# Moving the six groups of the transposed second matrix from batches 1 and 2 to batches 2 and 3

## The chip, the core and the metric

The kernel runs on one core of a Trainium2 chip. The time is the device time of one execution in microseconds (us); smaller is better. A core has the engines TensorE (PE), VectorE (DVE), ScalarE (ACT), GpSimd (POOL) and SyncE (SP, which issues most DMAs). Each works off its own queue in the order in which the program was written out; an instruction whose inputs are not there yet holds all behind it on that engine. The on-chip memories are SBUF and, for the results of matmuls, PSUM with 8 banks.

## The reference

```python
# 4 batches x 12 heads x 448 tokens x 64; scores are passed through a sigmoid, not a softmax
scores = (q @ k.T) / sqrt(64) - log(448);   x = sigmoid(scores) @ v        # x: 1792 tokens x 768
h = x @ w_in;   g = where(h > 0, h, exp(min(h, 0)) - 1);   x2 = g @ w_out   # w_in 768x2048, w_out 2048x768
logits = x2 @ w_gate                                                        # 8 experts, 224 tokens for each
for idx in argsort(-logits.flatten()):   # the largest logit takes its token, until an expert is full
    ...
out[tokens of e] = relu(x2[tokens of e] @ w1[e]) @ w2[e]
```

The choice of experts needs the logits of all tokens, so it can begin only when the last batch's are known.

## The kernel before

**Numbers.** Every fp32 operand of a large product is split into a high part `h` and a rest `l`, and a product is three matmuls (h with h, h with l, l with h). DVE makes the rest by a subtraction; the cast that makes the high part goes to ACT or DVE. The weights come as pairs of 32-bit words of fp64 numbers; a few bit operations on DVE and one scaling pass on ACT `join` a pair into one fp32 word.

**Stages.** The four batches (448 tokens each) go through `attention(b)`, `layer1(b)` and `layer2(b)`. The program issues `layer1(b)`, then `attention(b + 1)`, then `layer2(b)`, and the attention of the next batch is interleaved with both layers; behind `layer1(3)` there is no further attention. `layer1` has 16 steps f: the split of one block of `w_in` (128x768), 18 matmuls of 448 columns into one PSUM bank, then the elu of the result: `Exp` and `Tanh` on ACT, two operations on DVE of which the second is the last that reads the bank, then the split of the result into `gH` and `gL`. `layer2` has 6 blocks of 48 matmuls. In batch 0 the weights are joined and stored (`wcopy`); the later batches load the joined ones.

**The transposed second matrix.** For the last batch the logits are not taken from `x2` but earlier, from `gH` and `gL` and the product of `w_out` and `w_gate` (`wgs2`), in `last_logits()`. That product is built by `through(k)`, six groups for k = 0 to 5. A group loads two halves of `w_outT[k]` (1 MB each) into the two tiles `arena0` and `arena1`, joins each half in place, takes a bank from the ring of `layer1`, runs four fp32 products with `wgp` as the stationary operand (8 matmul records), and adds the bank to the accumulator `acc`. For each half:

```python
plan.dma(x, w_outT[k, hf])
V.tensor_scalar(lo, lo, 29, None, op0=ALU.logical_shift_right)
V.scalar_tensor_tensor(out=lo, in0=hi, scalar=-0x80000000, in1=lo, ...)
A.activation(f32(hi), f32(hi), AF.Copy, scale=2.0 ** -112)
V.tensor_scalar(hi, hi, 0x0FFFFFFF, 3, op0=ALU.bitwise_and, ...)
V.tensor_tensor(out=y, in0=hi, in1=lo, op=ALU.bitwise_or)
```

The last group (k = 5) is followed by four transposes into a further bank and the split into `wgs2`. The two arenas hold one group at a time, so the loads of the next group wait for the matmuls of the last. After the last group the arenas hold the tables of the expert search (`tables()`).

**Banks.** `mm` is a ring of three PSUM banks, 0, 1 and 2: each call gives the next in turn, to a step f, to a group, and to the transposes. A bank is written again only when what was in it has been read.

**What sets the order.** All operations are recorded, and a planner (`Plan.run`) writes out one queue for each engine: it takes operations by their estimated start and, where they could start together, by priority, which is the place in the program unless `plan.first(n)` moves it. The loads and joins of a group have `first(-300)`, which puts them behind their neighbours; `last_logits`, `tables`, `search` have `first(1e5)`. The order on the engines is fixed from then on.

Of the kernel before, what the change touches and what calls it, by code (L numbers as in the profile page):

```python
# [44 lines left out]
def f32(ap):  # L45
    return ap.bitcast(F32)
# [244 lines left out]
def kernel(  # L291
# [97 lines left out]
    def hcopy(dst, src):  # L389
        AV_.copy(dst, src)  # L390

    def lsub(dst, src, h):
        V.tensor_tensor(out=dst, in0=src, in1=f32(h), op=ALU.subtract)
# [68 lines left out]
    def through(k):  # L462


        ws = []
        for hf in range(2):
            x = r_raw()
            if wide:
                y = x.rearrange("p a b -> p (a b)")[:, :KH * P].rearrange("p (a b) -> p a b", b=P)
                lo, hi = (x.rearrange("p c (f two) -> p c f two", two=2)[:, :, :, i] for i in range(2))  # L470
                with plan.first(-300):
                    plan.dma(x, w_outT[k, hf])
                    V.tensor_scalar(lo, lo, 29, None, op0=ALU.logical_shift_right)
                    V.scalar_tensor_tensor(out=lo, in0=hi, scalar=-0x80000000, in1=lo, op0=ALU.bitwise_and,
                                           op1=ALU.bitwise_or)
                    A.activation(f32(hi), f32(hi), AF.Copy, scale=2.0 ** -112)
                    V.tensor_scalar(hi, hi, 0x0FFFFFFF, 3, op0=ALU.bitwise_and, op1=ALU.logical_shift_left)
                    V.tensor_tensor(out=y, in0=hi, in1=lo, op=ALU.bitwise_or)
                y = f32(y)
            else:  # L480
                y = x.rearrange("p a b -> p (a b)")[:, :KH * P].rearrange("p (a b) -> p a b", b=P).bitcast(F32)
                plan.dma(y, w_outT[k, hf])
            ws.append(y.rearrange("p a b -> p (a b)"))
        ps = mm()
        with plan.unit():
            for j in range(4):
                PE.matmul(ps[32 * j:32 * j + 32, :4 * P], wgp[:, k, :], ws[j // 2][:, j % 2 * 4 * P:(j % 2 + 1) * 4 * P],
                          start=True, stop=True)
        if k == 0:
            V.tensor_copy(acc, ps)  # L490
        else:
            V.tensor_tensor(out=acc, in0=ps, in1=acc, op=ALU.add)
        if k == KD - 1:
            ps = mm()
            with plan.unit():
                for c in range(4):
                    PE.transpose(ps[:, c * P:(c + 1) * P], acc[:, c * P:(c + 1) * P], ident)
            src = ps.rearrange("p (c j x) -> p j c x", j=4, x=32)[:, :, :, :E]
            w4 = wgs2.rearrange("p (j c) x -> p j c x", j=4)
            V.tensor_copy(w4[:, :, :, :E], src)  # L500
            lsub(w4[:, :, :, E:], src, w4[:, :, :, :E])

    def weights(b, r):

        n = KD if r < KF else KH
        src = w_in[r] if r < KF else w_out[r - KF]
        d = r_wd()
        if wide and b == 0:
            x = r_raw()
            plan.dma(x[:, :n], src)  # L510
            join(d[:, :n], x[:, :n], d[:, :n])
            plan.dma(wcopy[r, :, :n], d[:, :n])
        else:
            plan.dma(d[:, :n], wcopy[r, :, :n] if wide else src)
        h, l = r_wh(), r_wl()
        hcopy(h[:, :n], d[:, :n])
        lsub(l[:, :n], d[:, :n], h[:, :n])
        return h, l
# [65 lines left out]
    def layer1(b):  # L584
        ws = {}
        for f in range(-2, KF):
            with plan.first(200), plan.after(xs[0][GW + f][0]) if b == 0 and f < 1 else nullcontext():
                if f + 2 < KF:
                    ws[f + 2] = weights(b, f + 2)
            if f < 0:  # L590
                continue
            if b in (1, 2) and f in (1, 6, 11):
                through((b - 1) * 3 + f // 5)
            h, l = ws.pop(f)
            ps = mm()
            for c in range(KD):
                with plan.unit():
                    for n, (w, m) in enumerate(((h, 0), (h, 1), (l, 0))):
                        PE.matmul(ps[:, :S], w[:, c, :], xs[b][c][m], start=c == 0 and n == 0,
                                  stop=c == KD - 1 and n == 2)  # L600
            e, t = r_a(), r_a()
            A.activation(e, ps[:, :S], AF.Exp)
            A.activation(t, ps[:, :S], AF.Tanh, scale=0.5)
            V.scalar_tensor_tensor(out=t, in0=e, scalar=1.0, in1=t, op0=ALU.add, op1=ALU.mult)
            V.scalar_tensor_tensor(out=t, in0=t, scalar=0.0, in1=ps[:, :S], op0=ALU.min, op1=ALU.max)
            hcopy(gH[:, f, :], t)
            lsub(gL[:, f, :], t, gH[:, f, :])
# [82 lines left out]
    for b in range(B):  # L690
        plan.bias = BIAS[1] if b == 0 else {}
        layer1(b)
        if b == 0:
            plan.dma(wg, w_gate.rearrange("(d p) e -> p d e", p=P))
            V.tensor_copy(wgs[:, :, :E], wg)
            lsub(wgs[:, :, E:], wg, wgs[:, :, :E])
            V.memset(wgp, 0.0)
            V.tensor_copy(wgp[:, :, :E], wg)
        plan.bias = BIAS[2] if b == 0 else {}
        if b + 1 < B:  # L700
            attention(b + 1)
        layer2(b)
# [403 lines left out]
```

## Time and profile before

| | |
|---|---|
| median of 3 runs | 1009.49 us (1008.43 to 1009.92) |
| profiled execution | 1010.62 us, of it the span 1008.8 us |
| busy: PE, weight loads, DVE, ACT | 97%, 80%, 75%, 44% of the span |
| mean granted clock of TensorE | 0.990 |
| `layer1` of batch 3 on PE | 562.7 to 615.7 us |

The span runs from the first instruction to the last. A row that says "idle before, releaser" tells how long the engine stood in front of that work and which engine's work ended the wait. A matmul record is about 366 ns long in `layer1`, but the matmuls overlap, so that 261 of them take 53.17 us. The granted clock is 1.00 at full speed (2.4 GHz) and 0.50 at the lower level (1.2 GHz).

### The profile page before, as it was taken

How to read it: one execution, taken by the hardware profiler on the slowest of the kernel's cores; microseconds unless marked ns; L12 is line 12 of the kernel's file. 1: busy time of each engine (PE TensorE's matmuls, PEld its weight loads, DVE VectorE, ACT ScalarE, POOL GpSimd, SP SyncE). 2: the span in 40 equal slices, each digit the busy share in tenths (PEclk: the TensorE clock that was granted, in tenths of full speed). 3: DMA queues.
4: the chain of work that ended last, by engine and by line, in shares of the span. 5: the costliest groups of instructions: out<-in, count | busy, mean ns of one | idle time of the engine just before them, and what ended most of it. 6: DMA issues, size and time to landing. Idle time of an engine off the chain costs nothing. (4 is left out here: it accounts for less than half of the span.)

```text
span 1008.8 us, 15529 instructions
## 1 busy us (share of the span) xinstructions
PE 976.4 (97%) x6039; PEld 811.5 (80%) x6039; DVE 752.6 (75%) x1335; ACT 445.8 (44%) x631; POOL 45.6 (5%) x42
## 2 busy tenths in 40 slices
PE   8999999998999999899999999999899999999997
PEld 3497666786886698777678898888899989989997
DVE  5899977769996445997434687788798899798861
ACT  6779856446564412675320342133433244342320
POOL 0000000000000000000000000010011111102000
PEclk9999999999999999999999999999899999999999
DMA  7856767866452366433124333375555547456820
GB/s 218 294 201 237 264 229 265 271 230 213 175 203 86 115 171 198 164 115 111 63 79 138 113 115 105 120 252 185 174 208 174 187 137 278 163 168 239 282 89 28
DMA packets 63562, 177.99 MB, mean 176 GB/s; under 512 B 6336, under 2 KB 28096, under 8 KB 60416
## 3 DMA queue, kind: packets, MB, share of 16 engines
q1 hardware_dynamic: 60832, 165.98, 48.8%
q0 software_dynamic: 2656, 11.01, 3.5%
q8 instruction: 47, 0.77, 0.3%
q14 instruction: 27, 0.22, 0.1%
HBM read 147.87 MB, written 29.10 MB: 175 GB/s over the span
## 5 line engine op out<-in xcount | busy, mean ns | idle before, releaser
L247 PE MATMUL bank<-zone_r 128*128 128x448 f32 (+1 forms) x3384 | 633.7, 343 | 12.9 <-DVE zone L247 10.1
L247 PEld LDWEIGHTS bank<-zone_r 128*128 128x128 f32 x3384 | 556.3, 191 | 79.5 <-issue 20.6
L247 DVE TENSOR_TENSOR zone_r<-zone,zone_r 128x768 fp32r<-128x768 f32 (+3 forms) x347 | 314.3, 918 | 34.9 <-ACT zone_r L247 28.3
L247 PE MATMUL twin<-zone_r 128*112 128x384 f32 (+2 forms) x1416 | 226.2, 354 | 3.3 <-ACT zone L247 3.3
L247 PEld LDWEIGHTS twin<-zone_r 128*112 128x112 f32 (+2 forms) x1416 | 187.0, 175 | 33.4 <-issue 15.6
L247 ACT ACTIVATE zone_r<-zone 128x768 fp32r<-128x768 f32 (+3 forms) x194 | 151.6, 795 | 123.2 <-PE bank L247 48.6
L247 ACT ACTIVATE zone<-bank 128x448 f32<-128x448 f32 x156 | 79.5, 542 | 187.2 <-PE bank L247 161.0
L247 DVE CAST zone_r<-zone 128x768 fp32r<-128x768 f32 (+3 forms) x153 | 84.9, 557 | 91.0 <-PE bank L247 69.5
L247 ACT ACTIVATE zone<-twin,bias_s 112x896 f32<-112x896 f32 x96 | 92.8, 1005 | 61.5 <-PE twin L247 61.2
L247 PE MATMUL bank<-zone 112*64 112x448 f32 x384 | 83.9, 553 | 0.9 <-DVE zone_r L247 0.9
L247 ACT ACTIVATE zone_r<-bank 128x448 fp32r<-128x448 f32 x62 | 33.5, 544 | 111.5 <-PE bank L247 111.2
L247 DVE SCALAR_TENSOR_TENSOR zone<-arena,zone 128x768 int32<-128x768 int32 (+1 forms) x56 | 59.8, 1068 | 1.0
L247 PEld LDWEIGHTS bank<-zone 112*64 112x64 f32 x384 | 22.8, 136 | 37.7 <-issue 33.8
L247 DVE TENSOR_TENSOR arena<-m,arena 128x896 bf16<-128x896 f32 (+1 forms) x35 | 51.0, 1457 | 0.0
L247 ACT ACTIVATE zone<-twin 112x384 f32<-112x384 f32 (+2 forms) x48 | 24.7, 536 | 50.3 <-DVE zone L247 20.0
L247 DVE SCALAR_TENSOR_TENSOR zone<-zone 128x448 f32<-128x448 f32 x64 | 39.5, 618 | 2.5 <-ACT zone L247 2.5
L247 DVE SCALAR_TENSOR_TENSOR zone<-zone,bank 128x448 f32<-128x448 f32 x64 | 39.4, 616 | 1.0
L891 POOL DMA_INDIRECT zone<-x2rows,idx x18 | 24.2, 1343 | 340.6 <-PE bank L247 234.8
L247 ACT ACT_TABLE_LOAD x29 | 37.2, 1283 | 3.3 <-PE bank L247 1.6
L247 DVE CAST zone_r<-bank 128x448 fp32r<-128x448 f32 x13 | 8.1, 623 | 36.1 <-PE bank L247 36.1
L247 DVE TENSOR_TENSOR zone_r<-bank,zone_r 128x448 fp32r<-128x448 f32 x45 | 27.5, 618 | 3.1 <-ACT zone_r L247 2.7
L247 ACT ACTIVATE zone<-arena 128x768 f32<-128x768 f32 (+1 forms) x28 | 28.1, 1004 | 2.2 <-DMA arena<-w_out 1.3
(106 smaller groups left out, 365.9 us busy)
## 6 DMA issues: line engine op xcount, KB each, us to landing
zone<-we SPq DMA_DIRECT2D x64, 768.0 KB, 5.7
zone<-wcopy SPq DMA_DIRECT2D x48, 384.0 KB, 3.0
zone<-wcopy SPq DMA_DIRECT2D x36, 512.0 KB, 3.3
arena<-w_in SPq DMA_DIRECT2D x16, 768.0 KB, 4.7
arena<-w_out SPq DMA_DIRECT2D x12, 1024.0 KB, 5.9
arena<-w_outT SPq DMA_DIRECT2D x12, 1024.0 KB, 7.1
x2rows<-zone SPq DMA_DIRECT2D x48, 224.0 KB, 3.8
zone<-kq SPq DMA_DIRECT2D x23, 448.0 KB, 3.4
```

Of the source, the lines that this page charges most:

```text
L247: fn = lambda: getattr(self.eng[e], name)(*args, **kw)
L891: plan.add([("G", 1.05, lambda: plan.eng["G"].indirect_dma_start(**kw))], [plan.region(x) for x in reads], [plan.region(x) for x in writes ...
```

## The change

Before, the groups k = 0, 1, 2 stand in `layer1(1)` and k = 3, 4, 5 in `layer1(2)`, each time in front of the steps 1, 6 and 11. Now k = 0, 1, 2 stand in `layer1(2)` in front of the steps 1, 6 and 11, and k = 3, 4, 5 in `layer1(3)` in front of the steps 1, 4 and 7.

```diff
-            if b in (1, 2) and f in (1, 6, 11):
-                through((b - 1) * 3 + f // 5)
+            if (b, f) in ((2, 1), (2, 6), (2, 11), (3, 1), (3, 4), (3, 7)):
+                through((b - 2) * 3 + (f // 5 if b == 2 else f // 3))
```

On PE, in `layer1` of batch 1. `arena_77` and `arena_78` are the two arenas (a group's matmuls), `bank_70` to `bank_72` the three banks of the ring, `twin` the banks of attention. Before, from the second group on:

```order
L247 MATMUL bank_71<-zone_r 128x448 x18
L247 MATMUL bank_70<-zone_r 128x448 x18
L247 MATMUL bank_72<-arena_77,zone 32x512 x2
L247 MATMUL bank_72<-arena_78,zone 32x512 x2
L247 MATMUL bank_71<-zone_r 128x448 x18
L247 MATMUL bank_72<-zone_r 128x448 x18
```

Now, in the same batch:

```order
L247 MATMUL twin_75<-zone_r 112x448 x6
L247 MATMUL twin_74<-zone_r 112x448 x6
L247 MATMUL bank_70<-zone_r 128x448 x18
L247 MATMUL bank_71<-zone_r 128x448 x18
L247 MATMUL bank_72<-zone_r 128x448 x18
```

The groups are gone from there, and the steps take the banks in turn.

On PE, in `layer1` of batch 3, before (steps 0 to 4; three matmuls of step 2 stand further up):

```order
L247 MATMUL twin_75<-ident,zone 128x16 x3
L247 MATMUL bank_71<-zone_r 128x448 x9
L247 MATMUL bank_72<-zone_r 128x448 x18
L247 MATMUL bank_70<-zone_r 128x448 x15
L247 MATMUL bank_71<-zone_r 128x448 x18
L247 MATMUL bank_72<-zone_r 128x448 x18
```

Now, from step 4 to the end of step 10:

```order
L247 MATMUL bank_70<-zone_r 128x448 x18
L247 MATMUL bank_71<-zone_r 128x448 x18
L247 MATMUL bank_72<-arena_77,zone 32x512 x2
L247 MATMUL bank_72<-arena_78,zone 32x512 x2
L247 MATMUL bank_72<-zone_r 128x448 x42
L247 MATMUL bank_70<-arena_77,zone 32x512 x2
L247 MATMUL bank_70<-arena_78,zone 32x512 x2
L247 MATMUL bank_72<-zone_r 128x448 x9
L247 MATMUL bank_71<-ident,zone 128x128 x4
L247 MATMUL bank_70<-zone_r 128x448 x18
L247 MATMUL bank_71<-zone_r 128x448 x18
L247 MATMUL bank_72<-zone_r 128x448 x3
```

The group k = 4 stands behind steps 4 and 5. Behind it come 42 matmuls on bank 2 (steps 6 and 7, and 6 of the 18 of step 10), then the group k = 5, the transposes, and steps 8 and 9 on the other two banks.

On DVE, in the same stretch, a step before:

```order
L247 TENSOR_TENSOR zone_r<-zone,zone_r 128x768
L247 SCALAR_TENSOR_TENSOR zone<-zone 128x448
L247 SCALAR_TENSOR_TENSOR zone<-zone,bank_71 128x448
L247 CAST zone_r<-zone 128x448
L247 TENSOR_TENSOR zone_r<-zone,zone_r 128x448
```

Now, from the addition that empties the bank of k = 4 on:

```order
L247 TENSOR_TENSOR zone<-bank_72,zone 128x512
L247 CAST zone_r<-zone 128x768
L247 TENSOR_TENSOR zone_r<-zone,zone_r 128x768
L247 SCALAR_TENSOR_TENSOR zone<-zone 128x448
L247 TENSOR_SCALAR arena_77<-arena_77 128x1024
L247 SCALAR_TENSOR_TENSOR zone<-zone,bank_72 128x448
L247 SCALAR_TENSOR_TENSOR arena_77<-arena_77 128x1024
L247 TENSOR_TENSOR zone_r<-zone,zone_r 128x448
L247 TENSOR_SCALAR arena_77<-arena_77 128x1024
L247 TENSOR_SCALAR arena_78<-arena_78 128x1024
L247 TENSOR_TENSOR arena_77<-arena_77 128x1024
L247 SCALAR_TENSOR_TENSOR arena_78<-arena_78 128x1024
```

The first bit operation of k = 5 (on `arena_77`) stands between the two operations that empty bank 2 of step 6, and the rest of the join between those and the ones for step 7.

## Rows read from the trace of the kernel before

**Rows 1.** Engine totals of the page; engine, busy us, share, instructions.

```profile
PE 976.4 (97%) x6039; PEld 811.5 (80%) x6039; DVE 752.6 (75%) x1335; ACT 445.8 (44%) x631; POOL 45.6 (5%) x42
```

**Rows 2.** Stage table, batches 1 to 3: busy times, granted clock, DMA share.

```profile
225.00:285.00 60.00, 56.47 (x287) 44.56 (x287) 54.28 (x82) 39.92 (x56) 0.00 (x0) 0.97 0.52 177
388.00:450.00 62.00, 58.09 (x307) 45.91 (x306) 54.18 (x94) 37.64 (x56) 0.61 (x3) 1.00 0.51 170
562.00:616.00 54.00, 54.00 (x269) 49.59 (x268) 45.70 (x76) 23.32 (x42) 0.00 (x0) 1.00 0.36 116
```

**Rows 3.** PE timeline, `layer1` of batch 1: start, length, work, idle before.

```profile
244.18 3.95 PE L247 MATMUL bank<-zone_r 128*128 128x448 f32 x18 [1.15 <-DVE zone L247]
250.51 5.48 PE L247 MATMUL bank<-zone_r 128*128 128x448 f32 x18 [2.38 <-DVE zone L247]
```

**Rows 4.** PE timeline, `layer1` of batch 2.

```profile
417.39 2.06 PE L247 MATMUL bank<-zone_r 128*128 128x448 f32 x9 [2.85 <-DVE zone L247]
419.38 1.06 PE L247 MATMUL bank<-arena,zone 128*32 128x512 f32 x8
...
441.19 3.91 PE L247 MATMUL bank<-zone_r 128*128 128x448 f32 x18 [1.06 <-DVE zone L247]
445.03 1.75 PE L247 MATMUL bank<-arena,zone 128*32 128x512 f32 x8
```

**Rows 5.** PE timeline, `layer1` of batch 3.

```profile
558.69 0.55 PE L985 MATMUL twin<-idle 128*128 128x448 bf16 x2
...
562.72 53.17 PE L247 MATMUL bank<-zone_r 128*128 128x448 f32 x261
```

**Rows 6.** The twelve loads of `w_outT`, from issue to landing.

```profile
DMA to landing us min/median/max: 4.7/7.1/10.9
```

**Rows 7.** DVE timeline, pieces from batches 1 to 3.

```profile
240.95 1.22 DVE L247 SCALAR_TENSOR_TENSOR arena<-arena 128x1024 int32<-128x1024 int32 x1
242.08 0.95 DVE L247 TENSOR_TENSOR zone_r<-zone,zone_r 128x768 fp32r<-128x768 f32 x1
242.95 0.55 DVE L247 CAST zone_r<-zone 128x768 fp32r<-128x768 f32 x1
...
250.91 0.69 DVE L247 TENSOR_SCALAR arena<-arena 128x1024 int32<-128x1024 int32 x1
251.51 0.62 DVE L247 TENSOR_TENSOR zone_r<-zone,zone_r 128x448 fp32r<-128x448 f32 x1
252.04 0.61 DVE L247 SCALAR_TENSOR_TENSOR zone<-zone,bank 128x448 f32<-128x448 f32 x1
252.57 1.22 DVE L247 TENSOR_TENSOR arena<-arena 128x1024 int32<-128x1024 int32 x1
...
420.99 0.68 DVE L247 TENSOR_TENSOR zone<-bank,zone 128x512 f32<-128x512 f32 x1
...
450.35 0.39 DVE L247 CAST zone_r<-zone 128x448 fp32r<-128x448 f32 x1
...
566.84 0.62 DVE L247 SCALAR_TENSOR_TENSOR zone<-zone,bank 128x448 f32<-128x448 f32 x1
```

**Rows 8.** ACT by line and form, batches 1 and 2: the arena passes.

```profile
L247 ACT ACTIVATE arena<-arena 128x1024 f32<-128x1024 f32 x12 | 13.9, 1156 | 5.2 <-DVE arena L247 5.0
```

**Rows 9.** ACT timeline, batch 3: `Exp` and `Tanh` of one step.

```profile
564.85 0.98 ACT L247 ACTIVATE zone<-bank 128x448 f32<-128x448 f32 x2 [1.68 <-PE bank L247]
```

**Rows 10.** DVE timeline: first and last of the tables' instructions.

```profile
447.92 0.69 DVE L247 TENSOR_SCALAR arena<-arena 128x128 int32<-128x128 int32 x5
...
450.23 0.17 DVE L247 CAST arena<-arena 128x28 bf16<-128x28 int32 x1
```

**Rows 11.** Stage table of short stretches: clock behind idle times.

```profile
414.00:418.00 4.00, 1.15 (x6) 0.79 (x5) 4.00 (x8) 2.11 (x5) 0.00 (x0) 1.00 0.39 113
...
250.00:255.00 5.00, 4.49 (x15) 4.06 (x16) 4.42 (x7) 4.23 (x5) 0.00 (x0) 0.67 0.24 79
...
710.00:715.00 5.00, 5.00 (x24) 5.00 (x25) 3.49 (x6) 0.54 (x1) 0.00 (x0) 0.50 0.24 74
```

## The prediction

> **What bounds the kernel now.** I read the engine totals first: TensorE (PE) is busy 976.4 us of the 1008.8 us span [rows 1]. So time is lost only where PE stands idle or runs at a low clock, and the question is where that happens around the first layer, `layer1`, which the change touches. Stage tables give that next [rows 2]: in the stretch of batch 1 that holds three groups of the transposed second matrix, PE is busy 56.47 of 60 us; in the like stretch of batch 2, 58.09 of 62; in `layer1` of batch 3, which has no group, 54.00 of 54, with VectorE (DVE) at 45.70 and ScalarE (ACT) at 23.32. The PE timeline then names the holes. Batch 1 has two, 1.15 and 2.38 us, both ended by DVE, and the 18 matmuls behind the second take 5.48 us where the 18 behind the first take 3.95 [rows 3]. Batch 2 has 2.85 and 1.06 us, again ended by DVE, and one group of 8 matmuls that takes 1.75 us where another takes 1.06 [rows 4]. Batch 3 runs 261 matmuls in 53.17 us without a hole, 0.204 us each, 3.67 us for one step f of `layer1` [rows 5].
>
> So the groups cost PE time by what they make DVE do. The 8 matmuls of a group (1.06 us) are the same before and after; what matters is where DVE has no room, and whether PE has other work meanwhile. In batches 1 and 2 it has some: pieces of the next batch's attention. Batch 3 has no next batch.
>
> **What leaves batch 1.** Nothing of a group is left in its `layer1`, and the order there is plain steps of 18 matmuls rotating over three PSUM banks, as in batch 3 before. The two holes go, 1.15 + 2.38 = 3.53 us, and with them the slow 18 matmuls, 5.48 - 3.95 = 1.53 us [rows 3]: a gain of 5.1 us. The attention pieces that filled PE there move behind, among the matmuls of `layer2`, where they cost the same PE time. Bounds: 3.5 (only the holes) to 6.
>
> **Batch 2** has three groups at the same steps 1, 6 and 11 as before; only k is 0 to 2 instead of 3 to 5. Its holes stay: 2.85 + 1.06 us, and the 0.69 us of the slow group [rows 4]. I take 0, between -1.5 (the last group was followed by four transposes and the tables' DVE work, which now move) and +1.5.
>
> **What batch 3 gets.** The first of its groups (k = 3) is loaded and joined during the attention and `layer2` of batch 2, hidden as k = 3's was before. The other two must be loaded, joined and multiplied inside `layer1`, at steps 4 and 7: two arena buffers hold one group, so the DMAs of the next wait for the matmuls of the last. I follow the queues of the changed kernel from the end of step 0's matmuls, time 0, with durations from rows.
>
> *Up to the second group.* Group 3's matmuls end at 1.06. The loads of group 4 are issued then and land 7.1 us later in the median [rows 6], about 8.3. DVE works off its queue in order: between that landing and the second group's matmuls it holds 26 instructions, whose pace from start to start is 0.60 for a bit operation (TENSOR_SCALAR) on 1024 words, 1.13 for one with two inputs, 0.87 for a 768-wide subtraction, 0.53 for the 448-wide ones, 0.39 for a 448-wide cast [rows 7]. Sum: 4 x 0.60 + 4 x 1.13 + 4 x 0.87 + 12 x 0.53 + 2 x 0.39 = 17.5 us. ACT's two arena passes (1.16 each [rows 8]) lie beside it. So the second group can start at 8.3 + 17.5 + 0.2 = 26.0. PE has by then 1.06 + 5 x 3.67 + 0.4 (two short matmuls on the idle tile [rows 5]) = 19.8 us of work, for the order puts only steps 1 to 5 ahead of it. Idle: 6.2 us.
>
> On this sum the Trainium skill differs. VectorE: DVE Perf Modes, section "The DRAIN you can't avoid", says that the next instruction does not start until the pipe of the one before is empty; in these rows an unrelated next one starts about 0.08 us before the end of the record (0.61 long, 0.53 apart [rows 7]). By whole records the 26 would take 2.1 us more; the rows decide.
>
> *Between the second and the third group.* Three banks rotate. Group 4 takes bank 2, step 4 bank 0, step 5 bank 1, step 6 bank 2, group 5 bank 0, the transposes behind it bank 1, step 7 bank 2, steps 8, 9 and 10 banks 0, 1 and 2. Until group 5 is through, steps 8 and 9 are shut out, and the order shows what is left: 42 matmuls in a row on bank 2, that is steps 6, 7 and a third of step 10, each of which needs the bank emptied of the one before. First, step 6 waits for the addition that empties group 4: 0.68 us [rows 7] and two hand-overs, 1.0 us. It runs from 28.1 to 31.7. To empty it takes ACT 0.98 and DVE 2 x 0.62, 2.6 us when nothing is in the way (564.85 to 567.46 [rows 7, 9]). But in DVE's queue the first bit operation on group 5 stands between the two, and its load, issued at 27.1, lands at 34.3; with 0.60 and 0.62 behind it the bank is free at 35.6. Idle: 4.0 us. Step 7 ends at 39.3. Ahead of its emptying DVE has ten instructions, 7.7 us by the same paces, and 0.85 us of waiting for ACT's arena pass: 44.1. Idle: 4.85 us. The third group follows without a hole, and from step 8 the banks rotate again.
>
> Sum of the idle time: 6.2 + 1.0 + 4.0 + 4.85 = 16.1 us. Bounds: if loads land after 4.7 us [rows 6] and the two emptyings cost 2.6 each, about 11; if loads take 10.9 us, about 21.
>
> *What else moves.* The tables for the search, which need the arenas, are now built behind group 5: some 15 small DVE instructions; before they stand between 447.92 and 450.40, 2.5 us with two instructions of a step among them [rows 10]. They come when PE has steps 8 and 9 ahead of it (7.3 us), and the search needs them only after step 15. If that cover were gone, they would cost up to 2.5 us.
>
> *The clock.* After 2.38 us of idling with a short burst before it, the granted clock was 0.67 over 5 us; after 2.85 us alone it stayed at 1.00; at 710, behind a wait for the gathered rows, it was 0.50 over 5 us [rows 11]. Idles of 6.2, 4.0 and 4.85 us so close together should bring the lower of the two levels (1.2 of 2.4 GHz) at least twice. At 1.53 us each [rows 3] that is 3.1 us; bounds 0 and 2 x 2.5 = 5.0 from the row at 710, or more if it stays low all the way.
>
> *Sum.* -5.1 + 0 + 16.1 + 3.1 = +14.1 us. All later work hangs on PE's order behind `layer1` of batch 3, so nothing takes it back. The profiled execution took 1010.62 us (1.8 around its span), 1.1 above the median 1009.49; from it 1024.7, on the median 1023.6.
>
> **Rivals.**
> *The bank jam costs little (slower, +4 to +8, about 1016).* Loads land early, DVE's queue turns out shorter, both emptyings cost 2.6, and the clock holds: 11 - 5.1 = +6. For it: ACT has room. Against it: the 17.5 us of DVE do not depend on the loads' luck.
> The Trainium skill has a rule for the jam. Perfetto Trace Analysis, "Matmuls", wants independent groups to rotate through different PSUM banks so that emptying one overlaps the next; this order breaks it twice. By that rule alone the price is two bare emptyings, 2 x 2.6 instead of 4.0 + 4.85, and the sum +10.5. No row of before has two groups on one bank in a row.
> *The clock stays low from the second group to step 8 (+18 to +24, about 1031).* The work there, 2 x 1.06 + 3 x 3.67 = 13.1 us, would take up to twice as long, partly under DVE's work: 6 to 10 us more. For it: the 0.50 row [rows 11]. Against it: the batch 2 row with 1.00.
> *The holes only travel (about 1009.0, no change).* Batch 3 pays what batch 2 pays for its three groups, 4.6 us, against a gain of 5.1. Against it: there attention filled PE and the steps were 5 apart, here 3.
> *Faster: batch 3 has room (1004.4).* Without attention its DVE is free 54.0 - 45.7 = 8.3 us [rows 2], and ACT 30 us, to which casts can go. If the two joins (2 x 2 x (2 x 0.60 + 2 x 1.13) = 13.8 us), three additions (2.0) and the tables (2.5) fit, only the 5.1 us remain. It decides where DVE's free time plus the casts handed to ACT exceeds 18.3 us before step 8; but that free time is spread over 54 us, and the work stands in the first 46.
>
> **How the numbers follow.** Two us (0.2%) is about what a measurement can tell. Forecast (1018 to 1029): 0.62. Bank jam cheap: 0.13. Clock low: 0.14. Holes travel: 0.06, of it 0.04 within 0.2% and 0.02 slower. Faster: 0.05. So faster 0.05, same 0.04, slower 0.91. The range 1015 to 1031 leaves out the last two rivals and half of the clock's upper part.
>
> **What would show it.** In `layer1` of batch 1, no wait of PE for DVE. In that of batch 3, four waits ended by DVE: about 6 us in one or two pieces up to the second group's 8 matmuls, 1 behind them, then one in front of each 18 and 6 on the same bank, 4 and 5; the stage about 19 us longer; the clock below 1 there. DVE's first operation on group 5 should wait for its DMA. I am wrong if DVE idles while PE waits for the second group, if step 7 follows step 6 within 3 us, or if batch 1 keeps its holes.

## The result, and the profile after

The changed kernel takes 1021.72 us (median of 3 runs, 1021.29 to 1021.74) against 1009.49 before: ratio 1.0127, 95% interval 1.01 to 1.0155. It is slower by 12.2 us where 14.1 was forecast, and inside the range. The profiled execution took 1021.74, of which the span is 1019.9.

The engine totals, in the columns of [rows 1], tell little: PE is 6.0 us busier although it runs the same 6039 instructions, and it is the span that grew by 11.1.

```profile
PE 982.4 (96%) x6039; PEld 812.2 (80%) x6039; DVE 753.7 (74%) x1337; ACT 439.3 (43%) x623; POOL 45.1 (4%) x42
```

So the span is cut into stages. As marker I take PE's first small transposes (16x16) in the expert choice of each batch, a row that both traces have four times. These are the markers of batches 2 and 3 before, and then that of batch 3 after; that of batch 2 after is the first row of the timeline of batch 3 below.

```profile
562.44 0.35 PE L247 MATMUL twin<-ident,zone 16*128 16x16 f32 x3
631.45 0.42 PE L247 MATMUL bank<-ident,zone 16*128 16x16 f32 x4
...
643.64 0.42 PE L247 MATMUL bank<-ident,zone 16*128 16x16 f32 x4
```

| stage, us | before | after | difference |
|---|---|---|---|
| start to batch 0's marker | 221.41 | 219.62 | -1.79 |
| batch 0 to 1 (holds `layer1` of batch 1) | 170.86 | 162.15 | -8.71 |
| batch 1 to 2 (`layer1` of batch 2) | 170.17 | 169.90 | -0.27 |
| batch 2 to 3 (`layer1` of batch 3) | 69.01 | 91.97 | +22.96 |
| batch 3's marker to the end | 377.35 | 376.26 | -1.09 |

Work was moved between stages: three groups of 1.06 us left batch 1 and three came to batch 3, with four transposes (0.66 us) that came from batch 2. Without this moved work batch 1 gains 5.5 us, batch 2 loses 0.4, and batch 3 loses 19.1. Together this is 14.0. The first and the last line of the table have the same program in both kernels, but for three matmuls at the first marker. They differ by chance (the first is 219.62 in this trace of the changed kernel and 224.67 in its second one), and make 14.0 into the 11.1 of the two profiled executions.

The PE timeline of batch 1 after the change has, from the step of [rows 3] on, no hole (start, length, work, idle before in brackets):

```profile
226.37 51.34 PE L247 MATMUL bank<-zone_r 128*128 128x448 f32 x252
```

In batch 2 one hole with slow matmuls behind it is left of [rows 4], and 1.23 us for a group:

```profile
406.57 3.42 PE L247 MATMUL bank<-zone_r 128*128 128x448 f32 x9 [2.51 <-DVE zone L247]
409.93 1.23 PE L247 MATMUL bank<-arena,zone 128*32 128x512 f32 x8
```

Batch 3, where [rows 5] had one unbroken row of 261 matmuls, reads now:

```profile
551.67 0.35 PE L247 MATMUL twin<-ident,zone 16*128 16x16 f32 x3
...
552.75 1.06 PE L247 MATMUL bank<-arena,zone 128*32 128x512 f32 x8
553.75 11.42 PE L247 MATMUL bank<-zone_r 128*128 128x448 f32 x54
565.01 0.55 PE L985 MATMUL twin<-idle 128*128 128x448 bf16 x2
565.37 7.95 PE L247 MATMUL bank<-zone_r 128*128 128x448 f32 x36
573.25 1.05 PE L247 MATMUL bank<-arena,zone 128*32 128x512 f32 x4
578.00 1.92 PE L247 MATMUL bank<-arena,zone 128*32 128x512 f32 x4 [3.69 <-DVE arena L247]
580.80 5.53 PE L247 MATMUL bank<-zone_r 128*128 128x448 f32 x18 [0.89 <-DVE zone L247]
589.60 3.95 PE L247 MATMUL bank<-zone_r 128*128 128x448 f32 x18 [3.27 <-DVE zone L247]
598.06 2.58 PE L247 MATMUL bank<-zone_r 128*128 128x448 f32 x6 [4.50 <-DVE zone L247]
600.57 1.48 PE L247 MATMUL bank<-arena,zone 128*32 128x512 f32 x8
601.98 2.09 PE L247 MATMUL bank<-zone_r 128*128 128x448 f32 x9
603.91 0.60 PE L247 MATMUL bank<-ident,zone 128*128 128x128 f32 x4
604.26 23.78 PE L247 MATMUL bank<-zone_r 128*128 128x448 f32 x114
```

The reader is to see four things. Group 3 (552.75) goes through at once. Group 4 is cut in two, its first half at 573.25 and its second at 578.00. Behind it one step of 18, then another 18, then 6 stand alone, each with a hole ahead: these are the steps that share one bank. From 601.98 on the banks rotate again. The holes sum to 12.35 us. The rest of the 19.1, 6.7 us, is mostly in rows that take longer than they would, 5.2 us in those that stand out: 5.53 for 18 where 3.95 stands further down, 1.05 + 1.92 for a group in place of 1.06, 2.58 for 6 where three times 6 take 3.95, 1.48 for the last group. The tables of the search, which are built behind group 5, cost nothing here: PE has no hole behind 601.98.

The view of waits of the same stretch (who waits for whom: us in total, times, longest) shows the same four, all ended by DVE:

```profile
PE bank L247 <- DVE zone L247: 8.7, 3, 4.5
PE bank L247 <- DVE arena L247: 3.7, 1, 3.7
```

The table of 5-us stretches (busy time of PE, PEld, DVE, ACT, POOL, the granted clock, DMA share, GB/s) shows why rows take longer:

```profile
570.00:575.00 5.00, 4.31 (x21) 2.82 (x19) 5.00 (x8) 3.84 (x7) 0.00 (x0) 1.00 0.35 121
575.00:580.00 5.00, 1.92 (x4) 0.19 (x4) 3.51 (x7) 0.91 (x2) 0.00 (x0) 0.76 0.73 275
580.00:585.00 5.00, 4.20 (x13) 3.79 (x14) 0.66 (x1) 0.00 (x0) 0.00 (x0) 0.56 0.65 223
...
595.00:600.00 5.00, 1.94 (x5) 1.81 (x6) 4.59 (x7) 1.82 (x3) 0.00 (x0) 0.80 0.27 82
```

Behind the hole of 3.69 us the granted clock is 0.76 and then 0.56, near the lower of the two levels (1.2 of 2.4 GHz), and behind the later holes 0.80.

### The profile page after: what moved, and what is told of

The parts are those of the page before. It is cut to its first block, busy times and chain, and to the rows that moved or that the text cites. A ratio compares the mean times of both kernels' runs of the same rounds, so it can differ in the third digit from the quotient of the medians.

```text
span 1019.9 us, 15529 instructions
## 1 busy us (share of the span) xinstructions
PE 982.4 (96%) x6039; PEld 812.2 (80%) x6039; DVE 753.7 (74%) x1337; ACT 439.3 (43%) x623; POOL 45.1 (4%) x42
## 5 line engine op out<-in xcount | busy, mean ns | idle before, releaser
L247 ACT ACTIVATE zone_r<-zone 128x768 fp32r<-128x768 f32 (+3 forms) x196 | 155.4, 805 | 131.0 <-PE bank L247 60.3
L247 ACT ACTIVATE zone<-bank 128x448 f32<-128x448 f32 (+1 forms) x154 | 77.9, 540 | 184.0 <-PE bank L247 167.4
L247 DVE CAST zone_r<-zone 128x768 fp32r<-128x768 f32 (+3 forms) x151 | 82.6, 549 | 95.0 <-PE bank L247 70.4
```

The costliest lines, as they stand in the source:

```text
L247: fn = lambda: getattr(self.eng[e], name)(*args, **kw)
```

## The experiments

All ratios are to the kernel before, run on the same chip in the same rounds. Changes are shown against the changed kernel unless said otherwise. "Stage" is batch 2's marker to batch 3's: 69.01 us before, 91.97 after.

**The changed kernel again.**

> The changed kernel once more, unchanged, beside the kernel before on the same chip as the runs below. By the trace of its first profile it is about 12 us slower than the kernel before: between 1019 and 1023 if that one takes 1008 to 1009.

1022.68 us, ratio 1.013 (1.0109 to 1.0151). It confirms the result in other rounds, inside the 1019 to 1023 expected. Its holes are 3.70, 0.88, 3.27 and 3.96; in its profiled execution the low clock lasted longer, and the stage took 94.7. The holes are the order's; what the clock adds to them differs from one execution to the next.

**The groups of batch 3 on a bank of their own** (`av()` gives bank 3).

```
-        ps = mm()
+        ps = av() if k >= 3 else mm()
...
-            ps = mm()
+            ps = av()
```

> The changed kernel, but the groups k = 3, 4, 5 (batch 3) and the transposes take PSUM bank 3, which attention leaves free there, instead of a bank of the ring of three. DVE and ACT have exactly the same work. Theory (the bank jam and the place of the groups in PE's order make the holes): the holes behind the second group (0.9 + 3.3 + 4.5 us) go, the second group falls behind step 7 and so its 25 us of lag lie under steps, the clock stays up; 1021.7 - 12.4 - 6.6 = about 1003, at most 1007. Rival (DVE has more work than layer1 of batch 3 holds, whatever the banks): DVE's excess stays, PE waits elsewhere for it, 1015 or more.

1004.56 us, ratio 0.9953 (0.9936 to 0.9969): 17 us less than the changed kernel with the same loads, the same joins and the same steps. One more thing moved with the bank, against the expectation: the planner gave seven more casts of the stage to ACT, so that DVE runs 112 instructions there in 65.40 us and not 121 in 70.78. Its PE timeline of batch 3:

```profile
555.22 27.54 PE L247 MATMUL bank<-zone_r 128*128 128x448 f32 x132
582.69 1.06 PE L247 MATMUL bank<-arena,zone 128*32 128x512 f32 x8
583.68 28.78 PE L247 MATMUL bank<-zone_r 128*128 128x448 f32 x138
...
614.93 2.30 PE L247 MATMUL bank<-zone_r 128*128 128x448 f32 x10 [0.99 <-DVE zone_r L247]
617.15 1.06 PE L247 MATMUL bank<-arena,zone 128*32 128x512 f32 x8
```

The steps no longer wait for the groups: 132 of their matmuls run until group 4 starts at 582.69, counted from the marker some 3 us later than its second half in the changed kernel, and PE doesn't wait for it; group 5 comes at 617.15, in `layer2`. The stage is 76.45, a loss of 3.6 us beside the moved work in place of 19.1. So both joins fit into the stage, with seven casts handed to ACT, if PE is allowed to go ahead. The Trainium skill has this rule (Perfetto Trace Analysis, "Matmuls": independent groups rotate through different PSUM banks so that emptying one overlaps the next), and this run agrees with it: what broke the rotation was a group that holds its place in the ring while DVE works for it.

**The groups of batch 3 five steps apart instead of three.**

```
+            if b in (2, 3) and f in (1, 6, 11):
+                through((b - 2) * 3 + f // 5)
```

> The changed kernel, but the groups of batch 3 stand in front of steps 1, 6 and 11, as in batch 2, instead of 1, 4 and 7; the ring of three banks is kept. Theory (bank jam): with 5 steps between two groups only one pair of steps runs on one bank in a row (36 matmuls on bank 0 in front of the third group); one hole of 4 to 5 us there, 2 to 3 in front of the second group, some low clock: about 1011, between 1006 and 1015. Rival (DVE load alone): the same DVE work in the same layer1, so about 1021.

1014.48 us, ratio 1.0059 (1.0036 to 1.0081): inside the theory's 1006 to 1015, and half of the loss. The stage is 82.28, a loss of 9.4 us beside the moved work, with DVE as busy in it as in the changed kernel (70.80 us). Two holes are left of any size; the one expected in front of the second group is only 0.16 us:

```profile
598.34 5.81 PE L247 MATMUL bank<-zone_r 128*128 128x448 f32 x18 [4.61 <-DVE zone L247]
...
606.66 0.66 PE L247 MATMUL bank<-ident,zone 128*128 128x128 f32 x4 [1.52 <-DVE zone L247]
```

The first again stands between two steps on one bank, and the step behind it is slow (5.81). More distance makes the jam (a step that must wait for the bank of the step just ahead of it) rarer and does not remove it.

**The joins of groups 4 and 5 cut to one DVE operation per half** (three DVE operations and the ACT pass of each half are left out).

```
+                    if k >= 4:
+                        V.tensor_tensor(out=y, in0=hi, in1=hi, op=ALU.bitwise_or)
+                    else:
...
```

> The changed kernel with the join of the groups k = 4 and 5 cut to one bitwise operation on DVE for each half (it leaves out three DVE operations and the ACT pass of each half, so these two groups enter wgs2 with wrong numbers). Loads, matmuls, banks and places in the program are the same. Theory (DVE's queue in front of the second group, 17.5 us, is the first cause): it is 2 x 2.2 = 4.5 us shorter for each group, the order no longer has two steps on one bank in a row, the holes shrink to 3 us or less and the clock stays up: 1003 to 1007. Rival (the loads, 7.1 us from issue to landing between two groups, set the pace): holes of 4 us and more stay behind the second group, 1010 or more.

1009.1 us, ratio 0.9995 (0.9977 to 1.0014): between the two expectations. The direction is the theory's, the size is not. The loss of the stage beside the moved work is 6.2 us, about half of it in two holes:

```profile
582.45 1.05 PE L247 MATMUL bank<-arena,zone 128*32 128x512 f32 x4 [0.39 <-DVE arena L247]
586.24 1.48 PE L247 MATMUL bank<-zone_r 128*128 128x448 f32 x6 [2.74 <-DVE zone L247]
```

With hardly anything to join, PE doesn't wait for group 4 at all, and for the second half of group 5 only 0.39 us. But a bank is still used by two steps with only group 5 between, and there the hole is 2.74. It is not a bare emptying: the first of the two steps ended at 580.68, and DVE released its bank only at 586.19, because group 5's last bit operation, the split of the next `w_in` block and the tables of the search stood in its queue first. Its rows:

```profile
582.78 0.62 DVE L247 SCALAR_TENSOR_TENSOR zone<-zone 128x448 f32<-128x448 f32 x1
...
584.30 0.70 DVE L247 TENSOR_SCALAR arena<-arena 128x128 int32<-128x128 int32 x5
...
585.58 0.61 DVE L247 SCALAR_TENSOR_TENSOR zone<-zone,bank 128x448 f32<-128x448 f32 x1
```

So the tables, which cost nothing in the changed kernel, stand between the two operations of an emptying here for some 1.3 us. I had expected the short joins to free the order as well.

**Filler.** Three times 14 matmuls on the tile `idle`, which nothing reads, placed where the holes are.

```
+            if k >= 4 and hf == 0:
+                with plan.first(-2000):
+                    warm(14, twins[k % 2][:, 1], ws[0])
...
+            if k == 4:
+                with plan.first(-2000):
+                    warm(14, twins[0][:, 0], acc)
```

> The changed kernel with three times 14 matmuls on the idle tile added in layer1 of batch 3, into an unused bank; the planner sets them exactly in front of the second group's matmuls, between steps 6 and 7, and between step 7 and the part of step 10, that is into the holes. Theory (6.6 of the 19 us lost in this stage are the lower clock behind the holes): the holes stay, the granted clock stays at 1.00, the 18 matmuls of step 6 take 3.95 instead of 5.5 us: 1016 to 1018. Rival (the clock follows something else than PE's idling, or the added matmuls get in the way): 1021 or more.

1013.4 us, ratio 1.0062 (1.0038 to 1.0086): 8.3 us less than the changed kernel, although it computes more, and less than the 1016 to 1018 expected. Rows of its PE timeline, and one of its table of stretches:

```profile
579.94 3.95 PE L247 MATMUL bank<-zone_r 128*128 128x448 f32 x18 [1.26 <-DVE zone L247]
583.73 2.82 PE L385 MATMUL twin<-idle 128*128 128x448 bf16 x14
587.16 3.88 PE L247 MATMUL bank<-zone_r 128*128 128x448 f32 x18 [0.61 <-DVE zone L247]
...
595.05 1.46 PE L247 MATMUL bank<-zone_r 128*128 128x448 f32 x6 [1.35 <-DVE zone L247]
```

```profile
580.00:585.00 5.00, 5.00 (x25) 3.91 (x26) 1.17 (x2) 0.98 (x2) 0.00 (x0) 1.00 0.90 311
```

The step of 18 behind group 4 takes 3.95 at a granted clock of 1.00, where it took 5.53 at 0.56, and the six take 1.46 where they took 2.58. The stage is 87.02, that is 4.95 us less. In the four rows that were slow (the second half of group 4, the 18, the 6 and group 5) it is 4.0 us, and that much of the 6.7 is the clock's share; the rest of the 4.95 is in waits that ended earlier. The median gains more than the stage. In the profiled execution 6.5 us lie behind batch 3's marker (369.75 in place of 376.26). There PE waits for no gathered rows of `x2`, and the granted clock stays at 1.00, where the changed kernel's trace has this wait, up to 720.9 us, and a clock of 0.77 from 722 to 727:

```profile
PE twin L247 <- DMA zone<-x2rows,idx: 2.3, 1, 2.3
```

Whether the filler or chance did that, the runs do not settle.

**Batch 2's groups three steps apart, batch 1 and the rest as in the kernel before** (a change to that kernel).

```
-            if b in (1, 2) and f in (1, 6, 11):
-                through((b - 1) * 3 + f // 5)
+            if (b, f) in ((1, 1), (1, 6), (1, 11), (2, 1), (2, 4), (2, 7)):
+                through((b - 1) * 3 + (f // 5 if b == 1 else f // 3))
```

> The kernel before, with the groups of batch 2 in front of steps 1, 4 and 7 instead of 1, 6 and 11; batch 1 as before, no group in batch 3. The same density of groups as in the changed kernel's batch 3, but with the next batch's attention beside it, of which the planner sets two rounds between the second and the third group. Theory (it costs that much in batch 3 because PE has nothing else there): 2 to 6 us more than the kernel before, about 1012. Rival (density alone makes the price, 19 us against the 4.6 us of before): 1020 or more.

1014.44 us, ratio 1.0052 (1.0035 to 1.007), with 175.3 for batch 1 to 2 in place of 170.17. The largest hole:

```profile
409.64 7.30 PE L247 MATMUL bank<-zone_r 128*128 128x448 f32 x27 [2.68 <-DVE zone L247]
```

The closer order costs 5 us here, on top of the 4.6 us of holes and slow rows that the wider one already had there, so some 10 us. In batch 3, where there is no attention to run meanwhile, the wider order cost 9.4 and the closer one 19.1: attention beside the groups about halves the price of either.

**No load for group 5** (its matmuls use what the buffers hold).

```
-                    plan.dma(x, w_outT[k, hf])
+                    if k < 5:
+                        plan.dma(x, w_outT[k, hf])
```

> The changed kernel without the loads of the group k = 5; its join and matmuls work on what the arenas still hold (wgs2 gets wrong numbers). Every other instruction is kept. As nothing has to land, the planner sets four of the eight DVE operations of that join ahead of step 6's emptying, into the 5.5 us in which DVE stood idle; only two steps (6 and 10) stay on bank 2 in a row. Theory (two arenas hold one group, so load, join and matmuls of two groups stand strictly in line, and that line is part of the price): one hole of the three goes and the others shrink, 1021 - 5 to 8 us, 1012 to 1017. Rival (DVE's amount of work and the banks alone set it, the load lies under other work): within 2 us of the changed kernel.

1020.32 us, ratio 1.0114 (1.0087 to 1.0142): a miss of the 1012 to 1017, and near the rival's result: 1.4 us below the changed kernel's first median, 2.4 below that of the same rounds (1022.68), with intervals that overlap. The stage is 87.75, 4.2 us shorter than in the changed kernel's first trace, because the order changed too and one of the two jammed steps of 18 is gone; the other hole remains:

```profile
590.33 1.94 PE L247 MATMUL bank<-zone_r 128*128 128x448 f32 x6 [4.21 <-DVE zone L247]
```

As the order moved with it, the run doesn't isolate the load. The trace of the changed kernel says more on it (under step 7, below).

**Groups 3 to 5 left out.** Only k = 0 to 2 run, in batch 2 (a change to the kernel before).

```
-        if k == KD - 1:
+        if k == 2:
...
-            if b in (1, 2) and f in (1, 6, 11):
-                through((b - 1) * 3 + f // 5)
+            if b == 2 and f in (1, 6, 11):
+                through(f // 5)
```

> The first half of the change alone: groups k = 0, 1, 2 in batch 2, none in batch 1 and none in batch 3 (k = 3, 4, 5 are left out, so wgs2 is incomplete). It measures what leaving batch 1 gives back. Theory: 1009.5 less the holes and slow matmuls of batch 1 (5.1 us) less the 3 x 1.06 us of matmuls left out = 1001.2, within 1.5. Rival (the holes of batch 1 are only moved to where attention's matmuls now go): 1009.5 - 3.2 = 1006.3.

998.35 us, ratio 0.9898 (0.9861 to 0.9935), some 3 us below what was expected; the kernel before took 1008.57 in these rounds, so that the gain is 10.2 us in place of 8.3. Batch 0 to 1 takes 162.16, as in the changed kernel, and `layer1` of batch 3 is again whole:

```profile
555.21 53.17 PE L247 MATMUL bank<-zone_r 128*128 128x448 f32 x261
```

So the batch 1 gain and the batch 3 loss can be had apart. What it gains beyond that lies behind batch 3's marker (372.3 us to the end, against 377.35). There PE waits 1.2 us for the gathered rows in place of 3.3, and the low clock behind that wait [rows 11] is missing. The experts may also get other rows than before; the runs do not settle the cause.

**The six groups in `layer2` of batches 1 and 2**, on the banks of `sc()` (a change to the kernel before; the transposes take such a bank too).

```
-        ps = mm()
+        ps = sc()[:, 0]
...
-            if b in (1, 2) and f in (1, 6, 11):
-                through((b - 1) * 3 + f // 5)
...
+            if b in (1, 2) and d % 2 == 1:
+                through((b - 1) * 3 + d // 2)
```

> All six groups are taken out of layer1: k = 0, 1, 2 stand in layer2 of batch 1 and k = 3, 4, 5 in layer2 of batch 2, in front of blocks 1, 3 and 5, with a bank of the attention's ring. There DVE is busy some 9 of 20 us. Theory (the price of a group is DVE's lack of room in layer1 and the ring of three banks): the holes of batches 1 and 2 go, none come: the kernel before less 5.1 and 4.6 us, about 1000. Rival (a group costs PE holes wherever it stands, since its loads and joins are strictly in line): 1006 or more.

1002.91 us, ratio 0.994 (0.9925 to 0.9956). It lies between the expected 1000 and the rival's 1006. In the view of waits of the whole program, this is all that PE still waits for where DVE works in `zone`, the form of all the holes above but one:

```profile
PE bank L247 <- DVE zone L247: 1.1, 1, 1.1
```

That wait is in batch 0. So the holes of both kernels in `layer1` of batches 1 to 3 belong to the groups. Why it gains 6.0 us by the ratio (5.1 by the medians) and not the 9.7 that the stages promised stays open.

**Two groups in each of batches 1 to 3**, at steps 1 and 8 (a change to the kernel before).

```
-            if b in (1, 2) and f in (1, 6, 11):
-                through((b - 1) * 3 + f // 5)
+            if b and f in (1, 8):
+                through((b - 1) * 2 + f // 8)
```

> Two groups in layer1 of each of the batches 1, 2 and 3, in front of steps 1 and 8, with the ring of three banks. Only one group of each batch has to be joined inside layer1 (6.9 us of DVE), and 8 steps lie between the two. Theory: in batch 3 the order has no two steps on one bank in a row, at most 3 us of holes there, fewer holes than before in batches 1 and 2: 1001 to 1006. Rival (any group in batch 3 costs more than one in batches 1 and 2, as there is no attention): 1009 or more.

1007.64 us, ratio 0.9999 (0.9982 to 1.0015): a miss, above the 1001 to 1006 expected. The order used one bank for two steps on end once more, and this one place pays:

```profile
585.57 2.61 PE L247 MATMUL bank<-zone_r 128*128 128x448 f32 x6 [4.14 <-DVE zone L247]
```

**The same, with batch 3's two groups and the transposes on a bank of their own** (shown against the run before it).

```
-        ps = mm()
+        ps = av() if k >= 4 else mm()
...
-            ps = mm()
+            ps = av()
```

> Two groups in layer1 of each of the batches 1, 2 and 3 (steps 1 and 8), and those of batch 3 take PSUM bank 3 instead of one of the ring of three. The planner then sets k = 4 back into layer2 of batch 2 and k = 5 behind step 7, and no bank is used twice in a row. Theory: no hole over 1 us in batch 3, those of batches 1 and 2 as with two groups each: the kernel before less 6 to 9 us, about 1001. Rival (the hole of 4.1 us seen with two groups a batch is DVE's load and comes again elsewhere): 1006 or more.

1001.07 us, ratio 0.9918 (0.9898 to 0.9937): the fastest of those that leave nothing out, 0.8% faster than the kernel before and 2.1% faster than the changed one in the same rounds (1022.68). From 195 to 640 us the PE timeline has a single hole:

```profile
246.35 11.18 PE L247 MATMUL bank<-zone_r 128*128 128x448 f32 x54 [1.15 <-DVE zone L247]
```

The stage is 71.29, 0.6 us more than its moved work: the group k = 4 now stands ahead of the marker, so this is one group and the transposes.

## Why the prediction was right, and where it was not

**Batch 1: right.** -5.5 us against -5.1, and no wait for DVE is left there.

**Batch 2: right in the sum, not in its parts.** It loses 0.4 us where 0 was taken. I had its holes stay as they were; they changed (2.51 for 2.85 + 1.06), and as much as that gave back went to 9 slow matmuls (3.42 where 2.06 stood).

**Batch 3 up to the second group: right in kind, too large.** DVE's queue from the first operation on group 4 to the end of what the group needs:

```profile
560.30 0.69 DVE L247 TENSOR_SCALAR arena<-arena 128x1024 int32<-128x1024 int32 x1
...
576.73 1.22 DVE L247 TENSOR_TENSOR arena<-arena 128x1024 int32<-128x1024 int32 x1
577.86 0.61 DVE L247 TENSOR_TENSOR zone_r<-zone,zone_r 128x448 fp32r<-128x448 f32 x1
```

From 560.30 to 577.86 it works without a stop, 17.56 us where the paces gave 17.5; by whole records, as I had read the Trainium skill (VectorE: DVE Perf Modes, "The DRAIN you can't avoid"), it would have been 19.6. I had read it too strictly: the same section adds that a next operation that is not held starts earlier, and these rows, where the next one starts some 0.08 us before a record ends, agree with that. The second half of the group starts 25.3 us after time 0, foretold 26.0. The hole is 3.69 and not 6.2 because the first half, whose buffer is ready sooner, already ran at 573.25 (1.05 us), because PE's five steps ahead of it took 0.7 us longer, and because DVE began on the group some 0.75 us sooner than taken (560.30 is 7.55 us after time 0, foretold 8.3). I had treated the eight matmuls as one piece.

**The hand-over behind it: right** (0.89 against 1.0).

**Step 7: the hole is there, its cause was wrong.** I held that DVE waits for the load of group 5. The trace shows otherwise. The load of its first half was issued at 575.65, 1.4 us after the first half of group 4 had ended and freed that buffer:

```profile
575.65 4.64 SPq L278 DMA_DIRECT2D arena<-w_outT  x2
```

and DVE, in front of the step's emptying, stood idle for PE and not for a transfer:

```profile
586.16 0.56 DVE L247 CAST zone_r<-zone 128x768 fp32r<-128x768 f32 x1 [5.51 <-PE bank L247]
...
588.24 0.69 DVE L247 TENSOR_SCALAR arena<-arena 128x1024 int32<-128x1024 int32 x1
588.84 0.62 DVE L247 SCALAR_TENSOR_TENSOR zone<-zone,bank 128x448 f32<-128x448 f32 x1
```

The operation on group 5 (588.24) starts at the pace of its queue; the loads of groups 4 and 5 landed 4.6 to 7.9 us after their issue, so its data was there before. It costs the emptying 0.6 us and no more: the hole is the bare emptying, foretold at 2.6, and this one operation, 3.27 us in place of 4.0. It also came near the mark of 3 us at which I would have called myself wrong.

**Step 10's six: right.** 4.50 against 4.85, with DVE busy with group 5's bit operations ahead of the emptying.

**The clock: right in kind, too small.** The idle time was 12.35 us where 16.1 was foretold (by the terms as stated its bounds come to about 10 and 23, and not 11 and 21), and the slow rows 6.7 where 3.1 was. The two errors cancel by luck, so the stage's 19.1 against 19.2 flatters the working. The filler shows that some 4 us of the 6.7 are the clock; I had priced two low stretches by the one row at 250.51, and here the holes stood closer together. The rival in which the clock stays low was therefore nearer than its 0.14 said, though the time came out at the forecast. In the second trace of the changed kernel the holes are 11.81 us and the stage's other loss 10.1, about what that rival named; but its time of 1030.5 does not bear the rival out, since 5.0 us of what it is longer than the first trace lie ahead of batch 0's marker.

**The other rivals.** That the bank jam costs little is refuted: the two holes of the jam, 3.27 and 4.50, make 7.8 us against 5.2 for two bare emptyings and 8.85 foretold, and behind them comes the clock. The time alone would not tell: with two bare emptyings the sum was +10.5, which is as near to the 12.2 measured as the 14.1 is. That the holes only travel is refuted by batch 3's 19.1 against the 4.6 of batch 2 before. That batch 3 has room failed for this order, and was nearly right of the engines: with a bank of their own and seven more casts on ACT the same two joins fit into the stage, though the third group's matmuls then come in `layer2`.

Shown by runs: the loss of batch 3 needs two things together, a long queue on DVE in front of a group and a bank of the ring that the group holds meanwhile. Taking the groups out of the ring leaves 3.6 of the 19.1 us, cutting the joins short leaves 6.2. Distance, attention work and the clock change the price. Not shown apart: what of the own bank's gain comes from the casts that ACT took over with it, the price of the load alone, and the 6.7 us beyond the clock's 4.

## What to carry to other kernels

A group that waits long for a slow engine shouldn't take its place in a ring of buffers that fast steps share: most of its price here was not its own work but the steps behind it. Before moving work to a stage where an engine "has room", write down which buffer each step takes until the moved work is through, and look for two steps in a row on one. When holes cluster, price the clock from several close holes, and see whether work that nothing reads can keep it up.

## What the runs showed of the hardware that was not expected

Matmuls whose result nothing reads, in holes of 3 to 5 us, kept the granted clock at 1.00 where it had been 0.56 to 0.80, and the stage was 4.95 us shorter. And the same program differs much from one execution to the next: the kernel before ran from 1004.34 to 1012.93 us within one set of rounds. A trace is one execution, so a difference of 2 or 3 us between two traces outside the stage of an experiment could not be told from chance here.
